# Moving the streamed operand of TensorE against its next weights in SBUF: many distances in place of two

## The chip, the cores and the metric

The kernel runs on one core of one Trainium2 chip. The metric is the device time of one execution in microseconds (us). TensorE multiplies: it loads a block of 128x128 weights (`lhsT`, the trace's LDWEIGHTS, engine PEld) and streams columns of a second operand (`rhs`, the trace's MATMUL, engine PE) past it into PSUM. VectorE (DVE) and ScalarE (ACT) do the elementwise work, SyncE (SP) issues the transfers between HBM and SBUF.

## The reference

```python
def sm_attn(qq, kk, vv):
    s = scale * np.matmul(qq, kk.transpose(0, 1, 3, 2))
    a = np.exp(s - np.max(s, axis=-1, keepdims=True))
    return np.matmul(a / (np.sum(a, axis=-1, keepdims=True) + 1e-09), vv)
...
x = sm_attn(q, sm_attn(p, k, v), same)        # 8 batches, 8 heads, 576 tokens, 32 packs, head 64
x = x.reshape(4608, 512)
h = x @ w_in1                                 # 512 -> 2048
x = np.where(h > 0, h, np.exp(np.minimum(h, 0)) - 1) @ w_out1
h = x @ w_in2                                 # second MLP, 512 -> 2048 -> 512
P = a[0] + a[1]*h + a[2]*h**2 + a[3]*h**3
Q = 1 + abs(b[0])*abs(h) + abs(b[1])*h**2
out = (P / (Q + 1e-6)) @ w_out2
```

## The kernel before

Every large product is kept to float32 accuracy by splitting each operand into a high and a low part (float32r, four bytes each) and adding three matmuls: high x high, high x low, low x high. All those matmuls have a full 128x128 weight block of their own, so there is one weight load for each matmul.

**First MLP** (the first half of the time). Eight batches of 576 tokens, each in two halves of 288 (`TA`). A half's attention result lies in `A_flat` as a high and a low part (`s2_hi`, `s2_lo`); three such slots follow each other, one for each half in turn. For each of 16 blocks of 128 hidden units, `a_h` streams 288 columns of `A_flat` past blocks of the tile `m` (6 matmuls, line 395), the activation makes the two parts of `g` in one of two slots of `gl_all` (`a_hi`, `a_lo`), and `a_o` streams those past blocks of the tile `wo` (12 matmuls, line 430). A step of 18 matmuls repeats 256 times, 32 steps a batch. Between them stand the attention matmuls of the next batch.

**Second MLP** (the second half). The tokens are taken as 6 groups of 384 columns (`TU`), and for each group 8 pairs of hidden blocks: 48 pairs in all. A pair needs seven products of a two-by-two scheme with seven multiplications (`prod`, line 698, 6 matmuls each): it streams 384 columns of an operand in one of eleven x slots (`xslot`; 0 to 4 are parts of one tile, `xs_wi`; 5 to 10 are tiles of their own) past blocks of the tile `sw`. The rational function makes four `g` tiles for a pair (`g_tile`, in `A_flat` for even pairs, in `A_flat`, `g1`, `g2` and `g3` for odd ones). In `out_mm` (line 774, 36 matmuls a pair) these `g` tiles are the weights, and 512 columns of `wo2` are streamed. One window of the plan holds the products of one pair and the output matmuls of the one before.

The order on each engine is written out by hand (`PLAN`, `LAST` and the tables of steps), so it does not depend on the numbers below.

**Distances.** SBUF addresses here are counted in four-byte words within a partition. In the built program the weight tiles `m`, `wo`, `sw` and the streamed `wo2` start 48 words past a multiple of 64; `A_flat` and `gl_all` start 16 words past one. All strides inside (320 in `A_flat` and `gl_all`, 384 in x, 128 and 512 in the weights) are multiples of 64 words. So the distance from a streamed operand's start to the start of the next weights, counted modulo 64, is the same for all matmuls of a kind. The constants that set it before are

```python
TP, OFA, OFG = 320, 4, 4
OFX, OFM = 4, 28
```

`OFA` and `OFG` shift the operands in `A_flat` and `gl_all`: 16 + 4 - 48 = -28, which is 36 modulo 64. `OFX` shifts x: 48 + 4 - 48 = 4. `OFM` shifts the `g` tiles, which are weights: 48 - (16 + 28) = 4. Where the kind changes, the distance differs once: from a product to an output matmul it is 52 - 44 = 8, from an output matmul to a product 48 - 48 = 0.

Of the kernel before, what the change touches and what calls it, by code (L numbers as in the profile page):

```python
# [11 lines left out]
F32R = mybir.dt.float32r  # L12
# [10 lines left out]
def packed_attention_moe_moe2_kernel(  # L23
# [23 lines left out]
    TA = S // 2  # L47
    NBLK = TA // 32
    NU = NT // 2
    TU = 384  # L50
# [24 lines left out]
    NWS = NF - 1  # L75


    TP, OFA, OFG = 320, 4, 4
    OFX, OFM = 4, 28

    P = ctx.enter_context(tc.tile_pool(name="P", bufs=1))
    dram = ctx.enter_context(tc.tile_pool(name="dram", bufs=1, space=bass.MemoryType.DRAM))
# [4 lines left out]
    T2 = actx.enter_context(tc.tile_pool(name="T2", bufs=1))  # L87
# [9 lines left out]

    T2.tile([128, 32], F32, tag="pad", name="pad")
    A_flat = T2.tile([128, 12 * TP + 64], F32R, tag="A", name="A_flat")
    A_all = A_flat[:, :12 * TP].rearrange("p (a b c x) -> p a b c x", a=3, b=2, c=2)  # L100
    gl_all = T2.tile([128, 4, TP], F32R, tag="gl", name="gl_all")
    n_A = [0]

    ident = P.tile([128, 128], F32, tag="ident", name="ident")
# [227 lines left out]

    def s2_hi(b, hf):
        d = st[b]
        A = d["A", hf] = A_all[:, n_A[0] % 3, :, :, OFA:OFA + TA]
        n_A[0] += 1
        nc.scalar.copy(A[:, 0], d["s2y", hf])

    def s2_lo(b, hf, eng=None):
        d = st[b]  # L340
        A, y = d["A", hf], d.pop(("s2y", hf))
        (eng or nc.vector).tensor_tensor(A[:, 1], y, A[:, 0].bitcast(F32), ALU.subtract)

# [26 lines left out]
    wi = [wi_all[:, c] for c in range(NC)]  # L370
# [15 lines left out]
    def a_h(s):  # L386
        b, n, f, _ = a_step(s)
        m = m_t[b, f // 4]
        A = st[b]["A", n]
        ps = ps_w.tile([128, 512], F32, tag="h", name=f"h_{s}", bufs=2)  # L390
        c0 = (f % 4) * 128
        i = 0
        for r in range(2):
            for wx, ax in ((0, 0), (0, 1), (1, 0)):
                nc.tensor.matmul(  # L395
                    ps[:, :TA], lhsT=m[:, wx, r, c0:c0 + 128], rhs=A[:, ax, r, :],
                    start=(i == 0), stop=(i == 5))
# [13 lines left out]

    def a_hi(s):
        d = mlp[s]
        d["ghi"] = gl_all[:, s % 2, OFG:OFG + TA]
        nc.scalar.copy(d["ghi"], d["g"])  # L415

    def a_lo(s):
        d = mlp[s]
        d["glo"] = gl_all[:, 2 + s % 2, OFG:OFG + TA]
        nc.vector.tensor_tensor(d["glo"], d["g"], d["ghi"].bitcast(F32), ALU.subtract)  # L420

    acc = None
# [231 lines left out]
    swt, wo2, xs, bst = {}, {}, {}, {}  # L654
# [15 lines left out]
    def xview(t):  # L670
        return t[:, :4 * TU].rearrange("p (h k t) -> p h k t", h=2, k=2)

    def xslot(n, j):
        i = (7 * n + j) % 11
        if i not in xs:
            if i < 5:
                t = P.tile([128, 20 * TU + OFX], F32R, tag="wi", name="xs_wi")
                xs.update((k, xview(t[:, OFX + 4 * TU * k:])) for k in range(5))
            else:
                tag = "q" if i == 10 else f"m{i - 5}"  # L680
                xs[i] = xview(P.tile([128, 4 * TU + OFX], F32R, tag=tag, name=f"xs_{i}")[:, OFX:])
        return xs[i]

    def x_load(n, j):
        if n >= NB2:
            return
        nc.sync.dma_start(out=xslot(n, j).bitcast(F32), in_=x2d[:, j, :, :, n * TU:(n + 1) * TU].bitcast(F32))

    m2 = {}

    def prod(p, j, bank, start):
        if p >= NPAIR:
            return
        w, x = swt[p, j // 2], xslot(p // NPR, j)
        i = 0
        for k in range(2):
            for wx, xx in ((0, 0), (0, 1), (1, 0)):
                nc.tensor.matmul(  # L698
                    m2["ab"][bank][:, :TU], lhsT=w[:, j % 2, wx, k, :], rhs=x[:, xx, k, :],
                    start=(start and i == 0), stop=(i == 5), skip_group_check=True)  # L700
                i += 1
# [53 lines left out]

    def g_tile(p, f, i):
        k = 2 * (1 - f) + i
        a = A_flat[:, OFM:OFM + 12 * TP].rearrange("p (a x) -> p a x", x=2 * TU)
        if p % 2 == 0:
            return a[:, (2, 3, 4, 1)[k]]  # L760
        return (a[:, 0], m2["g1"], m2["g2"], m2["g3"])[k] if k else a[:, 0]

    def r_hi(p, f):
        nc.scalar.copy(g_tile(p, f, 0), m2["t", f])  # L764

    def r_lo(p, f):
        nc.vector.tensor_tensor(g_tile(p, f, 1), m2["t", f], g_tile(p, f, 0).bitcast(F32), ALU.subtract)

    def out_mm(p, i, fs=(1, 0), ks=(0, 1, 2)):
        for f in fs:  # L770
            w = wo2[p, f]
            for k in ks:
                g, wx = ((0, 0), (0, 1), (1, 0))[k]
                nc.tensor.matmul(  # L774
                    acc[i], lhsT=g_tile(p, f, g)[:, i * 128:(i + 1) * 128], rhs=w[:, wx, :],
                    start=(p % NPR == 0 and f == 1 and k == 0),
                    stop=(p % NPR == NPR - 1 and f == 0 and k == 2))
# [86 lines left out]
    with tc.manual_schedule():  # L864
# [51 lines left out]
        V, A = nc.vector, nc.scalar  # L916
# [20 lines left out]
        for f in range(NWS, NF):  # L937
            t = P.tile([128, 2, 512], F32, tag=f"wo{f}", name=f"scr_wo{f}")
# [43 lines left out]
        s2_pe(0, 1, extra("s2x"))  # L982
        s2_tr(0, 0)
        s2_hi(0, 0)
        m_lo(0, 0, half(0)[0])
        s2_lo(0, 0, V)
# [21 lines left out]
        def s2_at(s, *a):  # L1008
            seq_at(s, a, (s2_pe, s2_max), s2_sub, s2_exp, s2_sum, s2_mul, s2_tr, s2_hi, s2_lo)
# [15 lines left out]
        NS = 2 * NF  # L1025
# [9 lines left out]
        for t, fn, *a in ((-2, m_hi, 0, 0, h1), (-2, m_lo, 0, 0, h1), (-2, c3, oo[0]), (-2, c4, oo[0], nc.gpsimd),  # L1035
                          (-2, s2_max, 0, 1), (-2, s2_sub, 0, 1, V),
                          (-1, s2_exp, 0, 1), (-1, c3, oo[1]), (-1, s2_sum, 0, 1), (-1, s2_mul, 0, 1, V),
                          (-1, c4, oo[1], V),
                          (0, c3, oo[2]), (0, c4, oo[2], nc.gpsimd), (0, s2_tr, 0, 1), (0, s2_hi, 0, 1),
                          (0, s2_lo, 0, 1, V)):  # L1040
            at(ewq, t, fn, *a)
        for p in seq[NKD + 1:]:
            t = when[p]
# [14 lines left out]
        for b in range(B - 1):  # L1058
            o, n = b * NS, b + 1
# [33 lines left out]
        for i in range(4):  # L1093
            c, kt = divmod(i, 2)
            s = NS * (1 + i)
            a21, a22, a11, a12 = ("i", c + 2, kt), ("i", c + 2, kt + 2), ("i", c, kt), ("i", c, kt + 2)
            s1, s2, s3, s4 = (("s", i, j) for j in range(1, 5))
            ta, tb = ("cc", "cb") if i % 2 else ("cb", "cc")
# [21 lines left out]
        for i, (b, s, u, t) in enumerate(slots):  # L1120
            f = i // 2 + NPR * (i % 2)
# [3 lines left out]
        def b_open():  # L1125
            t1x.close()
            tb = t2x.enter_context(tc.tile_pool(name="TB", bufs=1, reuse_waits="tile"))
            for f in (1, 0):
                for t in ("w", "sq", "t"):
                    m2[t, f] = tb.tile([128, 2 * TU], F32, tag=f"{t}{f}", name=f"{t}_{f}")  # L1130
            for t in ("s1", "u2"):
                m2[t] = tb.tile([128, TU], F32, tag=t, name=t)
            m2["h1"] = tb.tile([128, 2, TU], F32, tag="h1", name="h1")
            m2["g3"] = tb.tile([128, 2 * TU + 32], F32R, tag="g3", name="g3")[:, OFM:OFM + 2 * TU]
            psm[0].close()
            ps_ab = psm[0].enter_context(
                tc.tile_pool(name="ps_ab", bufs=1, space=bass.MemoryType.PSUM, reuse_waits="tile"))
            m2["ab"] = [ps_ab.tile([128, 512], F32, tag=f"bank{i}", name=f"bank{i}") for i in range(2)]
            k = P.tile([128, 2 * TU + 3 * DM], F32, tag="k", name="h0_o")
            m2["h0", 0] = k[:, :2 * TU].rearrange("p (a t) -> p a t", a=2)  # L1140
            m2["o"] = [k[:, 2 * TU + DM * i:2 * TU + DM * i + DM] for i in range(3)]

        def b_rest():
            v = P.tile([128, 6 * TU + 32 + OFM], F32R, tag="v", name="xg_v")
            xs[9] = xview(v[:, OFX:])
            m2["g2"] = v[:, 4 * TU + 32 + OFM:]
            m2["g1"] = P.tile([128, 2 * TU + 32 + OFM], F32R, tag="wo15", name="g1")[:, 32 + OFM:]
            m2["h0", 1] = T2.tile([128, 2, TU], F32, tag="gl", name="h0")
            t = P.tile([128, 2, DM], F32, tag="wo14", name="o34")
            m2["o"] += [t[:, i] for i in range(2)]  # L1150
            acc[:0] = [ps_w.tile([128, 512], F32, tag="h", name=f"acc_h{i}", bufs=2) for i in range(2)]

        t2x = ExitStack()
        o = NA - NS
# [4 lines left out]
        for t in range(4):  # L1159
            at(ldq, o + 20 + t, s_load, 0, t)  # L1160
            at(ldq, o + 24 + t, s_load, 1, t)
        at(ldq, o + 24, b_open)
        for i in range(2):
            at(ldq, o + 26 + 2 * i, wo2_load, i)
# [3 lines left out]
        for s in range(-2, NA):  # L1168
# [13 lines left out]
            if 0 <= s + 1 < NA:  # L1182
                a_hi(s + 1)
                lo = functools.partial(a_lo, s + 1)
# [13 lines left out]
            if s >= 0 and a_step(s)[3][1] and a_evac(s):  # L1198
                prep, n = x_prep(s), a_step(s)[1] if s < NA - 1 else 2
                for i, ops in zip(XSTEPS[n][::2], XSTEPS[n][1::2]):  # L1200
                    for op in ops.split():
                        t = s + 1 + i
# [4 lines left out]
        for _ in mix:  # L1207
            pass
        run(ewq, NA)
        b_rest()  # L1210
        for s in range(NPAIR):
            for _ in window(s):
# [58 lines left out]
```

## Time and profile before

| what | value |
|---|---|
| median of 2 runs | 1491.83 us (1491.42 to 1492.24) |
| the profiled execution: its time / its span | 1491.81 us / 1490.0 us |
| mean granted TensorE clock | 0.998 of full speed (2.4 GHz) |
| matmuls with float32r operands: lines 430, 395, 698, 774 | 3072, 1536, 2016, 1728 |

The span runs from the first to the last instruction; the 1.8 us outside it are not in the trace. A matmul's busy time in the trace includes the time its columns need to pass through the array, and neighbours overlap; what a matmul costs is therefore read as the time from its start to the start of the next, from the start times of the timeline.

### The profile page before, as it was taken

The page shows a single profiled execution, that of the slowest core. Times are in us where ns is not written, and L with a number is a line of the kernel's source. Part 1 is how long each engine was busy: PE and PEld are TensorE (multiplying, and loading weights), DVE is VectorE, ACT ScalarE, POOL GpSimd, SP SyncE. Part 2 cuts the span into 40 slices and gives each one's busy share as a digit, 9 for nine tenths or more (in the row PEclk, how much of TensorE's full clock was granted, in tenths as well). Part 3 has the DMA queues.
Part 4 walks back from the last instruction along what each step waited for, and adds up shares of the span by engine and source line. Part 5 has one row for each costly group of instructions (what it writes and reads, how often), then busy time and mean ns, then how long its engine had stood idle before and what let it go on. Part 6 is the DMA issues. An engine that isn't in the chain of part 4 may idle for free.

```text
span 1490.0 us, 26768 instructions
## 1 busy us (share of the span) xinstructions
PE 1458.7 (98%) x10188; PEld 1325.0 (89%) x10188; DVE 1246.5 (84%) x2078; ACT 1087.1 (73%) x1992; POOL 3.3 (0%) x8
## 2 busy tenths in 40 slices
PE   7899999999999999999999999999999999999997
PEld 5778989999898999999989999999999999999996
DVE  6888687777877687776699999999999999999997
ACT  4876667676777667677778787787777778778775
POOL 0000000000000000000000000000000000000000
PEclk9999999999999999999999999999999999999999
DMA  9542555465555445467967877777677777777641
GB/s 355 177 150 62 172 149 169 127 184 154 154 164 157 149 146 162 137 204 236 326 193 258 296 226 254 259 233 236 223 257 237 249 262 223 257 257 226 203 143 56
DMA packets 191264, 301.14 MB, mean 202 GB/s; under 512 B 13472, under 2 KB 131488, under 8 KB 190240
## 3 DMA queue, kind: packets, MB, share of 16 engines
q1 hardware_dynamic: 190528, 298.51, 62.1%
q8 instruction: 81, 1.33, 0.4%
q10 hardware_dynamic: 608, 0.92, 0.2%
q14 instruction: 47, 0.39, 0.1%
HBM read 233.84 MB, written 65.54 MB: 201 GB/s over the span
## 4 chain that ended last, share of the span: by engine, by line
PE 85%; DMA 5%; DVE 5%; ACT 4%; issue 1%; SPq 0%; ACTq 0%; DVEq 0%
PE bank L698 23%; PE acc L430 22%; PE acc L774 17%; PE h L395 11%; PE acc_h L774 8%; PE m L351 2%; DMA x2d<-x 1%; DMA x2d<-xpart 1%; DMA raw0('o', 6)_134<-in_w_out_dram 1%; PE pp L252 1%; DVE g L410 1%; DMA raw0('o', 2)_118<-in_w_out_dram 1%; DMA s2d<-w2('i', 2, 2)_cb 1%; DMA v<-in_v_dram 1%; ACT g L405 0%
## 5 line engine op out<-in xcount | busy, mean ns | idle before, releaser
L430 PE MATMUL acc<-gl_all,wo 128*128 128x288 f32 x3072 | 454.1, 296 | 10.0 <-DVE gl_all L420 3.9
L430 PEld LDWEIGHTS acc<-gl_all,wo 128*128 128x128 f32 x3072 | 413.5, 188 | 54.0 <-ACT g L405 17.6
L395 PE MATMUL h<-A_flat,m 128*128 128x288 f32 x1536 | 242.9, 293 | 2.0 <-DVE m L365 0.9
L395 PEld LDWEIGHTS h<-A_flat,m 128*128 128x128 f32 x1536 | 214.9, 188 | 3.9 <-DVE m L365 1.6
L774 PE MATMUL acc<-wo,A_flat 128*128 128x512 f32 x768 | 200.8, 389 | 0.0
L698 PE MATMUL bank<-xs_wi,sw 128*128 128x384 f32 x960 | 191.3, 337 | 0.2 <-DVE h L716 0.2
L698 PE MATMUL bank<-xs,sw 128*128 128x384 f32 x912 | 180.9, 338 | 2.7 <-DVE h L716 2.6
L698 PEld LDWEIGHTS bank<-xs_wi,sw 128*128 128x128 f32 x960 | 171.2, 188 | 8.9 <-DVE h L716 0.7
L750 DVE SCALAR_TENSOR_TENSOR w<-w,sq 128x768 f32<-128x768 f32 x192 | 178.7, 950 | 0.1
L410 DVE SCALAR_TENSOR_TENSOR g<-g,h 128x288 f32<-128x288 f32 x256 | 115.7, 452 | 75.4 <-ACT g L405 73.3
L415 ACT CAST gl_all<-g 128x288 fp32r<-128x288 f32 x256 | 110.6, 432 | 90.2 <-PE acc L430 61.6
L698 PEld LDWEIGHTS bank<-xs,sw 128*128 128x128 f32 x912 | 162.6, 188 | 11.4 <-DVE h L716 3.7
L420 DVE TENSOR_TENSOR gl_all<-g,gl_all 128x288 fp32r<-128x288 f32 x256 | 115.6, 452 | 61.3 <-ACT gl_all L415 60.6
L774 PEld LDWEIGHTS acc<-wo,A_flat 128*128 128x128 f32 x768 | 142.5, 188 | 19.3
L404 ACT ACTIVATE g<-h 128x288 f32<-128x288 f32 x256 | 105.1, 411 | 48.4 <-PE h L395 47.9
L405 ACT ACTIVATE g<-g 128x288 f32<-128x288 f32 x256 | 113.9, 445 | 8.1
L774 PE MATMUL acc_h<-wo,A_flat 128*128 128x512 f32 x384 | 102.6, 390 | 0.0
L754 DVE SCALAR_TENSOR_TENSOR t<-t,cf,w 128x768 f32<-128x768 f32 x96 | 97.4, 1015 | 1.7
L732 DVE SCALAR_TENSOR_TENSOR w<-sq,cf,w 128x768 f32<-128x768 f32 x96 | 97.5, 1015 | 1.7
L743 ACT ACTIVATE sq<-w,cf 128x768 f32<-128x768 f32 x96 | 89.7, 934 | 1.6 <-DVE w L732 1.6
L746 ACT ACTIVATE sq<-sq,cf 128x768 f32<-128x768 f32 x96 | 89.7, 934 | 1.6
L764 ACT CAST A_flat<-t 128x768 fp32r<-128x768 f32 x72 | 60.4, 838 | 37.1 <-DVE t L754 37.0
(419 smaller groups left out, 1950.9 us busy)
## 6 DMA issues: line engine op xcount, KB each, us to landing
sw<-s2d SPq DMA_DIRECT2D x144, 512.0 KB, 4.2
wo<-wo2d SPq DMA_DIRECT2D x96, 512.0 KB, 5.1
x2d<-x SPq DMA_DIRECT2D x210, 144.0 KB, 2.4
xs_wi<-x2d SPq DMA_DIRECT2D x20, 768.0 KB, 7.5
xs<-x2d SPq DMA_DIRECT2D x19, 768.0 KB, 7.5
sw<-s2d SPq DMA_DIRECT2D x48, 256.0 KB, 2.8
q<-in_qT_dram SPq DMA_DIRECT2D x16, 576.0 KB, 5.5
v<-in_v_dram SPq DMA_DIRECT2D x8, 1024.0 KB, 6.7
```

What stands on the lines that cost most here:

```text
L395: nc.tensor.matmul(ps[:, :TA], lhsT=m[:, wx, r, c0:c0 + 128], rhs=A[:, ax, r, :], start=(i == 0), stop=(i == 5))
L404: nc.scalar.activation(d["e"], d["h"][:, :TA], AF.Exp)
L405: nc.scalar.activation(d["e"], d["e"], AF.Relu, scale=-1.0, bias=1.0)
L410: nc.vector.scalar_tensor_tensor(d["g"], d["e"], -1.0, d["h"][:, :TA], ALU.mult, ALU.max)
L415: nc.scalar.copy(d["ghi"], d["g"])
L420: nc.vector.tensor_tensor(d["glo"], d["g"], d["ghi"].bitcast(F32), ALU.subtract)
L430: nc.tensor.matmul(acc[m][:, :TA], lhsT=w[:, wx, m * 128:(m + 1) * 128], rhs=d[g], start=(first and i == 0), stop=(last and i == 2))
L698: nc.tensor.matmul(m2["ab"][bank][:, :TU], lhsT=w[:, j % 2, wx, k, :], rhs=x[:, xx, k, :], start=(start and i == 0), stop=(i == 5), skip_g ...
L732: nc.vector.scalar_tensor_tensor(w, m2["sq", f], cf[:, 5:6], w, ALU.mult, ALU.add)
L750: nc.vector.scalar_tensor_tensor(w, w, c, m2["sq", f], ALU.add, ALU.mult)
L754: nc.vector.scalar_tensor_tensor(t, t, cf[:, 0:1], m2["w", f], ALU.add, ALU.mult)
L774: nc.tensor.matmul(acc[i], lhsT=g_tile(p, f, g)[:, i * 128:(i + 1) * 128], rhs=w[:, wx, :], start=(p % NPR == 0 and f == 1 and k == 0), st ...
```

## The change

The four constants become tables. Nothing else changes: the built program has the same instructions in the same order on every engine, with the same waits, and all tiles start where they did; only the places of operands inside `A_flat`, `gl_all`, the x slots and the `g` tiles move, each by a multiple of 4 words.

```diff
-    TP, OFA, OFG = 320, 4, 4
-    OFX, OFM = 4, 28
+    TP = 320
+    OFA = (4, 12, 20, 32, 40, 44, 52, 60)
+    OFG = (4, 12, 20, 32, 24, 28, 16, 8)
+    OFX = (8, 12, 16, 20, 24, 28, 32, 36, 44, 52, 60)
+
+    def ofm(p):
+        return 4 * (p // 2 % 8) + (0 if p % 2 else 32)
...
-    gl_all = T2.tile([128, 4, TP], F32R, tag="gl", name="gl_all")
+    gl_all = T2.tile([128, 4 * TP], F32R, tag="gl", name="gl_all")
+
+    def A_part(b, i):
+        t = A_flat[:, OFA[b]:OFA[b] + 12 * TP].rearrange("p (a b c x) -> p a b c x", a=3, b=2, c=2)
+        return t[:, i, :, :, :TA]
+
+    def gl_part(s, i):
+        o = OFG[s // NS] + TP * i
+        return gl_all[:, o:o + TA]
...
-        A = d["A", hf] = A_all[:, n_A[0] % 3, :, :, OFA:OFA + TA]
+        A = d["A", hf] = A_part(b, n_A[0] % 3)
...
-        d["ghi"] = gl_all[:, s % 2, OFG:OFG + TA]
+        d["ghi"] = gl_part(s, s % 2)
...
-                t = P.tile([128, 20 * TU + OFX], F32R, tag="wi", name="xs_wi")
-                xs.update((k, xview(t[:, OFX + 4 * TU * k:])) for k in range(5))
+                t = P.tile([128, 20 * TU + OFX[4]], F32R, tag="wi", name="xs_wi")
+                xs.update((k, xview(t[:, OFX[k] + 4 * TU * k:])) for k in range(5))
...
     def g_tile(p, f, i):
         k = 2 * (1 - f) + i
-        a = A_flat[:, OFM:OFM + 12 * TP].rearrange("p (a x) -> p a x", x=2 * TU)
-        if p % 2 == 0:
-            return a[:, (2, 3, 4, 1)[k]]
-        return (a[:, 0], m2["g1"], m2["g2"], m2["g3"])[k] if k else a[:, 0]
+        o = ofm(p)
+        if p % 2 == 0 or k == 0:
+            o += 2 * TU * (0 if p % 2 else (2, 3, 4, 1)[k])
+            return A_flat[:, o:o + 2 * TU]
+        return m2[f"g{k}"][:, o:o + 2 * TU]
```

The distances modulo 64, in words:

| streamed, next weights | before | after |
|---|---|---|
| `A_flat`, `m` (line 395), batches 0 to 7 | 36 | 36, 44, 52, 0, 8, 12, 20, 28 |
| `gl_all`, `wo` (line 430), batches 0 to 7 | 36 | 36, 44, 52, 0, 56, 60, 48, 40 |
| x slots 0 to 10, `sw` (line 698) | 4 | 8, 12, 16, 20, 24, 28, 32, 36, 44, 52, 60 |
| `wo2`, `g` of even pairs 0, 2, 4, ... (line 774) | 4 | 0, 60, 56, 52, 48, 44, 40, 36, and again |
| `wo2`, `g` of odd pairs 1, 3, 5, ... | 4 | 32, 28, 24, 20, 16, 12, 8, 4, and again |

Together the rows of after hold all sixteen multiples of 4.

## Rows read from the trace of the kernel before

**Rows 1.** The page: busy time, share of the span and instructions of each engine.

```profile
PE 1458.7 (98%) x10188; PEld 1325.0 (89%) x10188; DVE 1246.5 (84%) x2078; ACT 1087.1 (73%) x1992; POOL 3.3 (0%) x8
```

**Rows 2.** Windows, all engines: busy us and instructions, then clock, DMA share, GB/s.

```profile
core 0: us, PE busy (x) PEld busy (x) DVE busy (x) ACT busy (x) POOL busy (x), PEclk, DMA share, GB/s
...
306.00:392.00 86.00, 86.00 (x793) 78.78 (x793) 66.08 (x149) 60.23 (x144) 0.00 (x0) 1.00 0.53 155
392.00:478.00 86.00, 86.00 (x796) 78.99 (x795) 66.19 (x149) 60.36 (x145) 0.00 (x0) 1.00 0.54 160
```

**Rows 3.** Windows of the second MLP, the same columns.

```profile
830.00:930.00 100.00, 100.00 (x504) 90.83 (x503) 92.72 (x111) 80.22 (x112) 0.00 (x0) 1.00 0.76 253
930.00:1030.00 100.00, 100.00 (x503) 90.85 (x503) 92.37 (x111) 76.71 (x108) 0.00 (x0) 1.00 0.72 238
...
1330.00:1430.00 100.00, 100.00 (x503) 90.92 (x503) 92.98 (x111) 78.35 (x110) 0.00 (x0) 1.00 0.69 227
```

**Rows 4.** Timeline of PE, first MLP: start us, us, engine, line, operation.

```profile
701.27 1.72 PE L430 MATMUL acc<-gl_all,wo 128*128 128x288 f32 x12
702.83 0.94 PE L395 MATMUL h<-A_flat,m 128*128 128x288 f32 x6
703.61 1.72 PE L430 MATMUL acc<-gl_all,wo 128*128 128x288 f32 x12
```

**Rows 5.** Timeline of PE, one window of the second MLP.

```profile
999.71 1.22 PE L698 MATMUL bank<-xs_wi,sw 128*128 128x384 f32 x6
1000.76 1.52 PE L774 MATMUL acc_h<-wo,A_flat 128*128 128x512 f32 x6
1002.13 1.22 PE L698 MATMUL bank<-xs_wi,sw 128*128 128x384 f32 x6
...
1006.95 2.27 PE L698 MATMUL bank<-xs,sw 128*128 128x384 f32 x12
1009.06 2.88 PE L774 MATMUL acc<-wo,A_flat 128*128 128x512 f32 x12
1011.78 1.22 PE L698 MATMUL bank<-xs,sw 128*128 128x384 f32 x6
...
1014.19 1.21 PE L698 MATMUL bank<-xg_v,sw 128*128 128x384 f32 x6
1015.25 1.04 PE L698 MATMUL bank<-xs_wi,sw 128*128 128x384 f32 x5
```

**Rows 6.** Timeline of PEld (weight loads), the same stretch.

```profile
1000.59 1.27 PEld L774 LDWEIGHTS acc_h<-wo,A_flat 128*128 128x128 f32 x6
```

**Rows 7.** Lines by form, PE: busy us, mean ns, idle us before.

```profile
L430 PE MATMUL acc<-gl_all,wo 128*128 128x288 f32 x3072 | 454.1, 296 | 10.0 <-DVE gl_all L420 3.9 <-ACT gl_all L415 2.7 <-ACT xpart L454 1.2
L395 PE MATMUL h<-A_flat,m 128*128 128x288 f32 x1536 | 242.9, 293 | 2.0 <-DVE m L365 0.9 <-ACT A_flat L337 0.7 <-DVE A_flat L342 0.5
L698 PE MATMUL bank<-xs,sw 128*128 128x384 f32 x912 | 180.9, 338 | 2.7 <-DVE h L716 2.6
```

**Rows 8.** Timeline of PE at a transpose of the attention (line 229).

```profile
153.33 0.60 PE L229 MATMUL t<-ident,E 128*128 128x128 f32 x4
153.76 0.27 PE L230 MATMUL t<-ident,E 128*64 128x128 f32 x1
```

More of the change, by code (lines that the diff above doesn't have):

```diff
@@ L99, in packed_attention_moe_moe2_kernel @@
     A_flat = T2.tile([128, 12 * TP + 64], F32R, tag="A", name="A_flat")
-    A_all = A_flat[:, :12 * TP].rearrange("p (a b c x) -> p a b c x", a=3, b=2, c=2)
-    gl_all = T2.tile([128, 4, TP], F32R, tag="gl", name="gl_all")
+    gl_all = T2.tile([128, 4 * TP], F32R, tag="gl", name="gl_all")
[5 more added lines that the diff above has]
+        return gl_all[:, o:o + TA]
     n_A = [0]
@@ L418, in a_lo @@
         d = mlp[s]
-        d["glo"] = gl_all[:, 2 + s % 2, OFG:OFG + TA]
+        d["glo"] = gl_part(s, 2 + s % 2)
         nc.vector.tensor_tensor(d["glo"], d["g"], d["ghi"].bitcast(F32), ALU.subtract)
@@ L676, in xslot @@
             if i < 5:
-                t = P.tile([128, 20 * TU + OFX], F32R, tag="wi", name="xs_wi")
-                xs.update((k, xview(t[:, OFX + 4 * TU * k:])) for k in range(5))
+                t = P.tile([128, 20 * TU + OFX[4]], F32R, tag="wi", name="xs_wi")
+                xs.update((k, xview(t[:, OFX[k] + 4 * TU * k:])) for k in range(5))
             else:
                 tag = "q" if i == 10 else f"m{i - 5}"
-                xs[i] = xview(P.tile([128, 4 * TU + OFX], F32R, tag=tag, name=f"xs_{i}")[:, OFX:])
+                xs[i] = xview(P.tile([128, 4 * TU + OFX[i]], F32R, tag=tag, name=f"xs_{i}")[:, OFX[i]:])
         return xs[i]
@@ L1133, in b_open @@
             m2["h1"] = tb.tile([128, 2, TU], F32, tag="h1", name="h1")
-            m2["g3"] = tb.tile([128, 2 * TU + 32], F32R, tag="g3", name="g3")[:, OFM:OFM + 2 * TU]
+            m2["g3"] = tb.tile([128, 2 * TU + 32], F32R, tag="g3", name="g3")
             psm[0].close()
@@ L1143, in b_rest @@
         def b_rest():
[L1144 to L1147, printed above, removed]
+            v = P.tile([128, 6 * TU + 128], F32R, tag="v", name="xg_v")
+            xs[9] = xview(v[:, OFX[9]:])
+            m2["g2"] = v[:, 4 * TU + 96:]
+            m2["g1"] = P.tile([128, 2 * TU + 64], F32R, tag="wo15", name="g1")[:, 32:]
             m2["h0", 1] = T2.tile([128, 2, TU], F32, tag="gl", name="h0")
```

## Prediction

> **What bounds the kernel now.** I read the shares of the engines first. TensorE is busy 98% of the span, its weight loads 89% [rows 1]. Since a busy TensorE can still hide waits, the windows come next: in two neighbouring stretches of the first MLP, and in every window of the second, PE is busy the whole time at granted clock 1.00, the 2.4 GHz level, while DVE has 66 of 86 us and 92 to 93 of 100 us [rows 2, 3]. The second MLP issues 503 or 504 matmuls in each 100 us whatever DVE and ACT do in them [rows 3]; the idle time before the two kinds of the first MLP is 12 us in all and before the products 2.7 us [rows 7]. So the time is a sum of matmul spacings, and what the change does to a spacing goes into the time one to one, with 12 to 15 us at most in which a slower matmul could fill a wait.
>
> The spacings come from the start times. First MLP: 18 matmuls from 701.27 to 703.61 are 2.34 us, 130.0 ns each [rows 4]. Products: 12 in 2.11 us and 6 in 1.05 or 1.06, 175 to 176.5 ns. Outputs: 12 in 2.72 us, 226.7 ns [rows 5]. From 288 to 512 columns the spacing grows by 96.7 ns, 0.43 ns a column; one column per cycle at 2.4 GHz is 0.417. So the columns take 120, 160 and 213 ns, and the rest, 10, 15.5 and 13.5 ns a matmul, is there beside each load. The load of the next weights does run beside the stream: the first load for the outputs starts at 1000.59, 0.17 us before the matmul that uses it at 1000.76, which is where the product before it starts [rows 5, 6]. This remainder is the only thing the change can act on through the distance.
>
> **The change part by part.** No instruction is added, removed or moved and no wait is new, so no transfer and no elementwise operation is later than before except by TensorE's own pace. The elementwise writes and the x transfers land at other places; 93 of 100 us of DVE are beside PE [rows 3], so a few per cent there would stay covered, and beyond 7% DVE would take over the second MLP. I cost them at nothing. What changes is the distance at 2,688 + 1,344 = 4,032 matmuls of the first MLP (seven of eight batches), at 2,016 products and at nearly all 1,728 outputs: 7,776 in all.
>
> What the trace says of other distances is little, but it is not nothing. The last product of a group that is followed by outputs has distance 8 where the others have 4: such a group of 6 takes 1.05 us, and the group of 6 followed by another product 1.06 [rows 5]. The last output before a product has distance 0 instead of 4: six take 1.37 us, twelve 2.72 us, 228 and 227 ns each [rows 5]. With one matmul in six different, a difference of more than some 10 ns in that one would show. So distances 0 and 8 cost what 4 costs, within 10 ns. Distance 36 is only seen at 288 columns, where the remainder is 10 ns, against 13.5 and 15.5 at 4. The other twelve distances are in no row.
>
> The bounds for these come from the two remainders. Above: the first MLP's matmuls take the product's 15.5 ns in place of 10, 5.5 ns x 4,032 = +22 us, and the second MLP, which is there already, stays. Below: the second MLP takes 10 ns, -5.5 ns x 2,016 - 3.5 ns x 1,728 = -17 us, and the first stays. That is 1514 and 1475 against the profiled execution's 1491.8, which is also the median of the runs to 0.02 us. I take half of each, since the new distances spread over all sixteen places and no row is nearer to one end: +11 - 8.5 = +2.5, **1494 us**.
>
> The Trainium skill's page "SBUF — State Buffer", section "Who interferes with whom", gives TensorE two independent read ports, one for the moving operand and one for weight loads, and says that TensorE never waits on anyone. By that rule the distance would be worth nothing and the sum would be 1491.8. The remainders above do not decide it: they show a cost beside the load, and not that it depends on the place.
>
> **The rivals.**
>
> *The place is worth nothing.* The remainder belongs to loading weights under a stream as such. For it: distances 0, 4 and 8 alike [rows 5], and spacings that repeat to 0.01 us through the half of the kernel in which three other engines write to SBUF. Against it: 10 ns at one distance and 13.5 to 15.5 ns at another, with nothing in the number of columns that would order them (288, 512, 384). Time: 1491.8, within 3. This is what the page's rule amounts to.
>
> *Sustained collisions.* Load and stream both walk through their words in order. If both take a word per cycle, a distance that puts them in the same part of the memory puts them there for the whole load, and they would take turns. The price: 128 words at 0.417 ns, 53 ns for each such matmul. For it: only four distances are seen, so twelve places could be bad. Against it: 0, where the two start at the same place modulo 64, shows nothing of the kind. If two of the sixteen distances are bad, 7,776 / 8 x 53 ns = +52 us, **1544**; if four, 1596. It decides from a mean of 3.8 ns over the 7,776, that is, from a little over one bad distance in sixteen. TensorE would be the place, and in the second MLP the bad ones would show as single x slots or single pairs.
>
> *Two distances that happen to be poor.* The remainder could be a collision already, absent elsewhere. For it: the transposes of the attention, whose distance is 48, take 0.43 us for 4, 108 ns each, where two cycles for each of their 128 columns are 106.7 [rows 8]. Against it: their loads are of another kind, and 0, 4, 8 and 36 all have the remainder. Going from 10, 15.5 and 13.5 to 2 ns would be worth 8 x 4,032 + 13.5 x 2,016 + 11.5 x 1,728 = 79 us at all distances, 40 at half of them: **1452**. DVE at 93% of the second MLP would still leave room for that [rows 3].
>
> The Trainium skill's page "TensorE: Matmul & The Clock Gate", section "Wait — 56ns, not 53.3ns?", puts the gap between streamed matmuls at the columns over 2.4 GHz plus about 2.5 ns. Its gaps here would be 122.5, 162.5 and 215.8 ns, all under the spacings of the trace; an estimate with that page's remainder at every changed matmul gives some 75 us less than now, 1417.
>
> *The change does not act as written*, for instance by a wait between operands that now overlap in `A_flat`. The built programs have the same waits, so this has next to no weight: 0.02.
>
> **How the numbers follow.** Mixed small effects, 1475 to 1514, 0.40: the forecast, 1494. The place is worth nothing, 1492: 0.25. Sustained collisions, 1515 to 1600 with most of it under 1550: 0.25. Poor places now, 1413 to 1475: 0.08. The last: 0.02. Two per cent of 1492 are 30 us, which is about what a measurement of this kernel can tell from no change. Faster by more than that (below 1462) needs most of the poor-place case: 0.07. Slower (above 1522) has nearly all of the collisions and some of the odd case: 0.26. Within: 0.67. The range for 8 in 10 runs from 1475, where the lower bound ends, to 1545, the collisions at two places: it leaves out the poor-place case and about half of the collisions.
>
> **What the profile of the changed kernel would show.** Batch 0 of the first MLP keeps its distances, so its step must stay at 2.34 us; if it does not, the cause is not the distance. With the forecast, the steps of the batches lie between 2.32 and 2.44 us (129 to 135.5 ns), groups of six products between 1.02 and 1.06 us, of six outputs between 1.34 and 1.37, and each x slot keeps its own value in all 48 windows. If the place is worth nothing, all of these are as before and windows take 15.53 us. With collisions, a few batches, slots or pairs stand out by tens of ns a matmul (a step of up to 3.3 us, a group of six products of up to 1.37) and the others stay. With poor places now, some fall to about 2.20 us a step. The forecast is wrong if the mean over the sixteen places is far from the places in use, in either direction: four distances seen of sixteen are a thin base, and that is its weakest step.

## The result: 1% slower

The changed kernel takes 1506.66 us (median of 2 runs, 1506.05 to 1507.27) against 1491.83 us: a ratio of 1.0102, 95% interval 1.0085 to 1.0118. That is inside the range of the prediction and within 2%; the forecast of 1494 had the sign and too small a size. The profiled execution took 1507.27 us with a span of 1505.5 us, 15.5 us more than the one of before.

The page's line of the engines, after the change, has the same instruction counts as [rows 1], with 17 us more in PE, 0.1 us in DVE and 1 us in ACT:

```profile
PE 1475.5 (98%) x10188; PEld 1334.1 (89%) x10188; DVE 1246.6 (83%) x2078; ACT 1088.2 (72%) x1992; POOL 3.3 (0%) x8
```

Windows of the second MLP after the change (busy us and instructions of PE, PEld, DVE, ACT, POOL, then the clock):

```profile
842.00:942.00 100.00, 100.00 (x499) 90.05 (x498) 91.96 (x110) 77.44 (x108) 0.00 (x0) 1.00 0.73 246
942.00:1042.00 100.00, 100.00 (x498) 89.97 (x497) 90.90 (x109) 77.25 (x108) 0.00 (x0) 1.00 0.70 237
```

PE is as full as in [rows 3], at the same granted clock, but issues 498 or 499 matmuls in 100 us in place of 503 or 504. The timeline of PE after the change: first a step's end in batch 0, whose distances are as before, then a whole step of batch 2 (distance 52), the first products of the second MLP, and a part of one window of the second MLP:

```profile
118.13 1.72 PE L444 MATMUL acc<-gl_all,wo 128*128 128x288 f32 x12
119.69 0.94 PE L409 MATMUL h<-A_flat,m 128*128 128x288 f32 x6
...
253.29 0.96 PE L409 MATMUL h<-A_flat,m 128*128 128x288 f32 x6
254.09 1.76 PE L444 MATMUL acc<-gl_all,wo 128*128 128x288 f32 x12
255.69 0.96 PE L409 MATMUL h<-A_flat,m 128*128 128x288 f32 x6
...
725.06 1.37 PE L712 MATMUL bank<-xs_wi,sw 128*128 128x384 f32 x7
...
1015.88 1.56 PE L789 MATMUL acc<-wo,A_flat 128*128 128x512 f32 x6
1017.27 2.28 PE L712 MATMUL bank<-xs,sw 128*128 128x384 f32 x12
1019.39 2.93 PE L789 MATMUL acc<-wo,A_flat 128*128 128x512 f32 x12
1022.15 1.22 PE L712 MATMUL bank<-xs,sw 128*128 128x384 f32 x6
```

The first product before the change; then groups of matmuls of one form (count, busy us, mean ns, idle us before), one of the outputs before, and both kinds of the first MLP, the same outputs and one group of products after:

```profile
717.46 1.22 PE L698 MATMUL bank<-xs_wi,sw 128*128 128x384 f32 x6
```

```profile
L774 PE MATMUL acc<-wo,A_flat 128*128 128x512 f32 x768 | 200.8, 389 | 0.0
```

```profile
L444 PE MATMUL acc<-gl_all,wo 128*128 128x288 f32 x3072 | 461.5, 299 | 8.1 <-ACT gl_all L429 2.8 <-DVE gl_all L434 2.3 <-ACT xpart L468 1.2
L409 PE MATMUL h<-A_flat,m 128*128 128x288 f32 x1536 | 245.9, 295 | 2.0 <-DVE m L379 0.9 <-ACT A_flat L351 0.7 <-DVE A_flat L356 0.5
L789 PE MATMUL acc<-wo,A_flat 128*128 128x512 f32 x768 | 204.6, 394 | 0.0
L712 PE MATMUL bank<-xs,sw 128*128 128x384 f32 x912 | 181.1, 338 | 2.5 <-DVE h L730 2.5
```

In batch 0 twelve matmuls take 1.56 us, 130.0 ns each, as in [rows 4]. In batch 2 a step is 2.40 us, 133.3 ns each. In the second MLP twelve products take 2.12 us, 176.7 ns, against 175.8 [rows 5]; twelve outputs 2.76 us, 230.0 ns, and six 1.39 us, 231.7 ns, against 226.7 [rows 5]. So the time came in two nearly equal parts: the first product starts 7.6 us later (725.06 against 717.46 us), and the rest, 8 us, is 0.16 us more for each of the 48 windows of the second MLP. The first of the two numbers is uncertain by some 2 to 3 us: in the seven profiled executions of this document that leave the first MLP as it was, the first product starts between 715.2 and 720.2 us. By the groups, the two kinds of the first MLP take 7.4 and 3.0 us more busy time than in [rows 7] and this group of outputs 3.8 us more, while the products take 0.2 us more. Products cost nothing; it is the steps of the first MLP and the outputs.

### The profile page after: what moved, and what is told of

Same layout as the page of the kernel before. It is cut to its first block, busy times and chain, and to the rows that moved or that the text cites. A ratio compares the mean times of both kernels' runs of the same rounds, so it can differ in the third digit from the quotient of the medians.

```text
span 1505.5 us, 26768 instructions
## 1 busy us (share of the span) xinstructions
PE 1475.5 (98%) x10188; PEld 1334.1 (89%) x10188; DVE 1246.6 (83%) x2078; ACT 1088.2 (72%) x1992; POOL 3.3 (0%) x8
## 4 chain that ended last, share of the span: by engine, by line
PE 87%; DVE 5%; ACT 4%; DMA 3%; issue 1%; SPq 0%; ACTq 0%; DVEq 0%
PE acc L444 23%; PE bank L712 22%; PE acc L789 17%; PE h L409 11%; PE acc_h L789 9%; PE m L365 2%; DMA x2d<-x 1%; PE pp L266 1%; DMA q<-in_qT_dram 1%; PE s1h L200 1%; DVE g L424 0%; DMA raw0('i', 0, 1)_99<-in_w_in_dram 0%; DMA wo2d<-whi('o', 10)_7848 0%; PE s L300 0%; DVE w L764 0%
## 5 line engine op out<-in xcount | busy, mean ns | idle before, releaser
L444 PE MATMUL acc<-gl_all,wo 128*128 128x288 f32 x3072 | 461.5, 299 | 8.1 <-ACT gl_all L429 2.8
L444 PEld LDWEIGHTS acc<-gl_all,wo 128*128 128x128 f32 x3072 | 419.8, 189 | 52.3 <-ACT g L419 18.4
L789 PE MATMUL acc<-wo,A_flat 128*128 128x512 f32 x768 | 204.6, 394 | 0.0
L768 DVE SCALAR_TENSOR_TENSOR t<-t,cf,w 128x768 f32<-128x768 f32 x96 | 97.4, 1015 | 1.7
L746 DVE SCALAR_TENSOR_TENSOR w<-sq,cf,w 128x768 f32<-128x768 f32 x96 | 97.4, 1014 | 1.6
```

Source lines behind the costliest of these rows:

```text
L444: nc.tensor.matmul(acc[m][:, :TA], lhsT=w[:, wx, m * 128:(m + 1) * 128], rhs=d[g], start=(first and i == 0), stop=(last and i == 2))
L746: nc.vector.scalar_tensor_tensor(w, m2["sq", f], cf[:, 5:6], w, ALU.mult, ALU.add)
L768: nc.vector.scalar_tensor_tensor(t, t, cf[:, 0:1], m2["w", f], ALU.add, ALU.mult)
L789: nc.tensor.matmul(acc[i], lhsT=g_tile(p, f, g)[:, i * 128:(i + 1) * 128], rhs=w[:, wx, :], start=(p % NPR == 0 and f == 1 and k == 0), st ...
```

## The experiments

Three theories of a matmul's spacing were open. **Distance**: it depends on the distance of the matmul's own kind. **Place**: it depends on where an operand starts, whatever the other does. **Neighbours**, later called carry-over: it also depends on what ran before it. A spacing in what follows is the mean over the matmuls named, from start times; means over a whole kernel leave out the few spacings with a wait in them.

**Everything 8 words further, distances kept.**

```diff
+    P.tile([128, 8], F32, tag="pad0", name="pad0")
     ident = P.tile([128, 128], F32, tag="ident", name="ident")
```

> The kernel before with one pad of 8 words ahead of all tiles: every operand lies 8 words further, all distances stay (36 and 4). Distance theory: the time of before, ratio within 0.2% of 1, steps of 130.0 ns and outputs of 226.7 ns. Place theory (what counts is where each operand starts, not how they stand to each other): a changed kernel's cost, a ratio of 1.005 to 1.015, outputs at 230 ns or more.

1491.36 us against 1491.89, ratio 0.9996 (0.9986 to 1.0005). Its timeline of PE:

```profile
701.83 1.72 PE L431 MATMUL acc<-gl_all,wo 128*128 128x288 f32 x12
703.39 0.94 PE L396 MATMUL h<-A_flat,m 128*128 128x288 f32 x6
704.17 1.72 PE L431 MATMUL acc<-gl_all,wo 128*128 128x288 f32 x12
...
1040.82 2.88 PE L775 MATMUL acc<-wo,A_flat 128*128 128x512 f32 x12
1043.54 0.69 PE L699 MATMUL bank<-xs,sw 128*128 128x384 f32 x3
```

A step is 2.34 us and twelve outputs are 2.72 us, the numbers of [rows 4, 5]. Where the operands lie is worth nothing as long as all move together by 8 words; the place theory falls for such a shift.

**A map of distances**, a kernel of nothing but matmuls with their loads, twelve in a group; DVE and ACT are idle beside them.

```diff
+    for n, d in ((288, 320), (512, 512)):
+        for iw in range(16):
+            for ix in range(16):
...
+                for m in range(4):
+                    for wx, g in ((0, 0), (0, 1), (1, 0)):
+                        w0, x0 = 4 * iw + 512 * wx + 128 * m, 4 * ix + d * g
+                        nc.tensor.matmul(t[:, :n], lhsT=W[:, w0:w0 + 128], rhs=X[:, x0:x0 + n], ...
```

> Leaves out the whole computation: only groups of 12 matmuls with their weight loads, streamed start and weights start each at all sixteen multiples of 4 words, once with 288 and once with 512 columns. Distance theory: all groups with the same difference cost the same, some 130 to 134 ns (288) and 227 to 234 ns (512), and the lowest of 288 is at difference 36, of 512 at 4. Place theory: rows or columns of the map agree and diagonals do not. Neighbour theory (the added cost comes from changing between distances): with one distance through a group, all groups alike within 1 ns.

Timeline of PE in the map; in a name like `s_n_e`, `s` is 288 columns (`l` 512), the next letter the streamed start in steps of 4 words (a = 0, n = 52), the last the weights' start (e = 16, f = 20, j = 36). The last group, `l_h_j`, is shown in its two halves, and then the start of the one after it:

```profile
136.08 1.77 PE L67 MATMUL s_l_e<-X,W 128*128 128x288 f32 x12
137.69 1.76 PE L67 MATMUL s_m_e<-X,W 128*128 128x288 f32 x12
139.29 1.73 PE L67 MATMUL s_n_e<-X,W 128*128 128x288 f32 x12
140.85 1.76 PE L67 MATMUL s_o_e<-X,W 128*128 128x288 f32 x12
...
163.02 1.72 PE L67 MATMUL s_m_f<-X,W 128*128 128x288 f32 x12
164.58 1.76 PE L67 MATMUL s_n_f<-X,W 128*128 128x288 f32 x12
...
836.94 2.91 PE L67 MATMUL l_f_j<-X,W 128*128 128x512 f32 x12
839.69 2.96 PE L67 MATMUL l_g_j<-X,W 128*128 128x512 f32 x12
842.49 1.56 PE L67 MATMUL l_h_j<-X,W 128*128 128x512 f32 x6
843.89 1.52 PE L67 MATMUL l_h_j<-X,W 128*128 128x512 f32 x6
845.25 2.88 PE L67 MATMUL l_i_j<-X,W 128*128 128x512 f32 x12
```

Twelve matmuls at distance 28 (`s_l_e`) take 1.61 us, 134 ns each; at 36 (`s_n_e`) 1.56 us, 130. With the weights 4 words further, the same distance (`s_m_f`, 48 - 20 = 28) takes 1.56 us, 130 ns. So distance 28 costs 134 ns with weights at a multiple of 8 words and 130 ns with weights 4 words past one. With 512 columns and weights at 36, a streamed start at 24 (`l_g_j`, distance 52) takes 2.80 us, 233 ns, and one at 20 (`l_f_j`, distance 48) 2.75, 229. This holds over the whole map: groups with the same distance and the same remainder of the weights' start by 8 words mostly agree to half a ns once the first two rows of weights are over, and the two remainders give two different lists. The place theory falls, as it wanted rows or columns of the map to agree, and so does a cost of changing distances alone, as groups that hold one distance each still differ by up to 8 ns. By medians of these, 288 columns take 130.2 (distance 36) to 134.1 ns (28) with weights at multiples of 8, and 130.1 (28) to 133.3 (36) with the others; 512 columns 227.2 (60) to 234.9 (52), and 226.7 (28 and 60) to 233.3 (52), with 228.1 at 4, where the lowest was expected. The lists are not those of the distance alone, though. In the map a group follows one whose distance is 4 less, always the same one but for the first of each row of weights, and the group `l_h_j` (distance 56) takes 1.40 us for its first six, 233.3 ns each, and 1.36 us for its last six, 226.7 each. The same fall stands in every group of 512 columns at distances 40 and 56 with weights 4 words past a multiple of 8, so the 230 ns that the lists have at these two is in part what ran before. Neither list goes below 130 and 226.7 ns. So the remainder over the columns, 10 and 13.5 ns, is not removed at any of them; the distances of before sit on the floor of the list in the first MLP and near it for the outputs.

**The table of the g tiles alone**, and **the tables of the first MLP alone** (the other tables set back to the constants of before).

```diff
-    OFA = (4, 12, 20, 32, 40, 44, 52, 60)
-    OFG = (4, 12, 20, 32, 24, 28, 16, 8)
-    OFX = (8, 12, 16, 20, 24, 28, 32, 36, 44, 52, 60)
+    OFA = (4,) * 8
+    OFG = (4,) * 8
+    OFX = (4,) * 11
```

> Only the table of the g tiles is changed, all else as before. Distance theory: outputs at some 232 ns as in the changed kernel, +8 us, ratio 1.0055; products and first MLP as before. Neighbour theory, with the x slots as the neighbours that count: outputs stay under 229 ns, ratio under 1.002.

1500.86 us, ratio 1.0064 (1.0049 to 1.0079): +9 us; outputs at 232.0 ns in the mean of their starts (227.0 before), products at 175.4, the first MLP at 130.0. Outputs under 229 ns, which the neighbour theory wanted, did not come.

```diff
-    OFX = (8, 12, 16, 20, 24, 28, 32, 36, 44, 52, 60)
+    OFX = (4,) * 11
...
-        return 4 * (p // 2 % 8) + (0 if p % 2 else 32)
+        return 28
```

> Only the two tables of the first MLP are changed. Distance theory: the steps of batches 1 to 7 as in the changed kernel, 131 to 134 ns a matmul, +8 us, ratio 1.0055, the second MLP as before. Neighbour theory: batches 1 to 3, in which both operands of a step have the same distance, fall back to 130 ns, and only batches 4 to 7 stay above; +4 us.

1499.21 us, ratio 1.005 (1.0035 to 1.0065): +7.3 us. Batch 2, where both operands have distance 52, is at 133 ns here too, and batches 1 and 3 at 131.4 to 131.8; so different neighbours are not needed for a cost.

**The x slots' table alone**, the part for which the changed kernel's products showed no cost.

```diff
-    OFA = (4, 12, 20, 32, 40, 44, 52, 60)
-    OFG = (4, 12, 20, 32, 24, 28, 16, 8)
+    OFA = (4,) * 8
+    OFG = (4,) * 8
...
-        return 4 * (p // 2 % 8) + (0 if p % 2 else 32)
+        return 28
```

> Only the table of the x slots is changed. Distance theory: products as in the changed kernel, 173 to 177 ns by slot and 175 in the mean, outputs at 227 ns, so no change: ratio 0.999 to 1.001. Neighbour theory: outputs above 229 ns because the products beside them have other distances, +4 us or more, ratio over 1.002.

1496.25 us, ratio 1.0032 (1.0022 to 1.0041), +5 us, which the distance theory excluded. Products stay at 175.5 ns; the outputs, whose own distance is 4 as before, rise to 229.3. Its timeline of PE from 1228.0 to 1232.6 us:

```profile
1228.55 2.91 PE L789 MATMUL acc<-wo,A_flat 128*128 128x512 f32 x12
1231.30 1.22 PE L712 MATMUL bank<-xs_wi,sw 128*128 128x384 f32 x6
```

and the same stretch of the same kernel from 1229.7 us on, which keeps the last eight of the twelve:

```profile
1229.48 1.98 PE L789 MATMUL acc<-wo,A_flat 128*128 128x512 f32 x8
```

The first four outputs after the products take 0.93 us, 232.5 ns each; the last eight 1.82 us, 227.5 each. This group is a marked one: over all 45 groups of twelve outputs in this run the first four take 230.2 ns and the last eight 228.0. The run `x16_g0` further on, with one place for all products and one for all outputs, shows it with nothing mixed; here is one of its groups of twelve, as three and nine:

```profile
1225.93 0.85 PE L789 MATMUL acc<-wo,A_flat 128*128 128x512 f32 x3
1226.62 2.20 PE L789 MATMUL acc<-wo,A_flat 128*128 128x512 f32 x9
1228.66 1.20 PE L712 MATMUL bank<-xs_wi,sw 128*128 128x384 f32 x6
```

The first three take 0.69 us, 230 ns each, and the other nine 2.04 us, 226.7 each; over its 45 such groups the first four spacings are 229.2, 232.5, 230.8 and 226.7 ns, and all later ones 226.6 or 226.7. So a group of outputs starts slow after products at another distance and comes to its own value after three or four matmuls; in the map it took six. A matmul's spacing carries over.

**Whose weights?** The second part of another map alternates the weights between two places 8e words apart and keeps the distance 36 either to a matmul's own weights (`o`) or to the next (`n`); its first part maps the products.

```diff
+                for k in range(24):
+                    w0 = (8 * e) * (k % 2)
+                    x0 = (w0 if own else 8 * e - w0) + 36
```

> Leaves out the whole computation. First part: the products' order of six matmuls with 384 columns, streamed start and weights start each at all sixteen multiples of 4 words, 12 matmuls a group. Distance theory: spacing set by the difference and by whether the weights start at a multiple of 8 words, between some 172 and 178 ns, with the difference 4 near 175.5 and at least one under 174. Second part: 24 matmuls with 288 columns, weights alternating between two places 8e words apart (e = 0 to 7). In groups o the streamed start keeps 36 words to its own weights, in groups n to the next weights. If the next weights count: n groups all at 130 to 130.5 ns, o groups at 132 to 133 for e of 1 to 3. If a matmul's own weights count: the other way round. If neither, both alike.

Timeline of PE (the letter after `o` or `n` is e, a = 0; the last one counts the two rounds):

```profile
583.58 3.39 PE L79 MATMUL n_b_a<-X,W 128*128 128x288 f32 x24
586.81 3.36 PE L79 MATMUL n_c_a<-X,W 128*128 128x288 f32 x24
590.00 3.29 PE L79 MATMUL n_d_a<-X,W 128*128 128x288 f32 x24
593.13 3.36 PE L79 MATMUL n_e_a<-X,W 128*128 128x288 f32 x24
...
609.08 3.29 PE L79 MATMUL o_b_b<-X,W 128*128 128x288 f32 x24
612.20 3.37 PE L79 MATMUL o_c_b<-X,W 128*128 128x288 f32 x24
615.41 3.35 PE L79 MATMUL o_d_b<-X,W 128*128 128x288 f32 x24
...
634.44 3.39 PE L79 MATMUL n_b_b<-X,W 128*128 128x288 f32 x24
637.67 2.56 PE L79 MATMUL n_c_b<-X,W 128*128 128x288 f32 x18
```

`n_b` takes 3.23 us (134.6 ns) in both rounds and `n_d` 3.13 (130.4), though the distance to the next weights is 36 in both; `o_b` takes 3.12 (130.0) and `o_c` 3.21 (133.8), though the distance to their own weights is 36. Neither distance alone sets the spacing; the two rounds agree to 0.2 ns, so it is not chance. In the first part the products lie between 173.2 (distance 28) and 179.0 ns (60) with weights at multiples of 8, and 4 costs 175.0.

**A map of combinations.** Products and outputs in the kernel's order, 48 matmuls for each pair of an x place and a g place, counted from the start of the weights and of `wo2`; the kernel before has x at 4 and g at 60.

```diff
+    for ig in range(16):
+        for ix in range(16):
...
+            for np_, no in ((2, 2), (1, 1), (1, 1)):
+                for j in range(np_):
+                    six(t, 4 * ix, j)
+                for j in range(no):
+                    outs(u, 4 * ig, j + np_)
```

> Leaves out the whole computation. Products and outputs of the second MLP in groups of 12, 12, 6, 6, 6, 6, in the kernel's order of operands, one x place and one g place for a group of 48, all 256 combinations. If spacing belongs to each kind's own distance: the products' mean depends on the x place alone and the outputs' on the g place alone, each by one column of numbers, within 0.5 ns. If a matmul's delay carries over into the next ones: outputs of the same g place differ by 2 ns and more with the x place, as they did in the run with the x table alone, and the place of before (x at 4, g at 60) gives 175.4 and 227.0 ns. A combination under 174 and at most 227 ns would beat the places of before by some 3 us in the kernel.

Timeline of PE: the first row of a group of 48 and the first of the group after it, for x at 56 and g at 0, for x at 60 and g at 32, and for the places of before:

```profile
152.11 2.25 PE L70 MATMUL p_o_a<-X,W 128*128 128x384 f32 x12
...
161.73 1.06 PE L70 MATMUL p_p_a<-X,W 128*128 128x384 f32 x5
...
1414.79 2.31 PE L70 MATMUL p_p_i<-X,W 128*128 128x384 f32 x12
...
1424.64 0.69 PE L70 MATMUL p_a_j<-X,W 128*128 128x384 f32 x3
...
2371.93 2.27 PE L70 MATMUL p_b_p<-X,W 128*128 128x384 f32 x12
...
2381.60 0.69 PE L70 MATMUL p_c_p<-X,W 128*128 128x384 f32 x3
```

The groups take 9.62, 9.85 and 9.67 us. Without the first six products of each group, whose neighbours belong to the group before, and scaled to 42 products and 36 outputs in 48 windows, the places of before give 747.1 us, the mean of all 256 combinations 754.0, the best (x at 56, g at 0: 173.9 and 226.9 ns) 742.6, the worst 766.6. With g at 0 the outputs lie between 226.5 and 231.3 ns by the x place alone: carry-over again. For the places of before the map has 175.3 and 227.9 ns, where 175.4 and 227.0 were expected from the kernel: its outputs are 0.9 ns too slow there.

**Three combinations put into the kernel**, all with the first MLP of before.

```diff
-    OFX = (4,) * 11
+    OFX = (56,) * 11
...
-        return 28
+        return 32
```

The second has 16 in place of 56; the third has 60, and returns 0.

> Distances of before in the first MLP; products all at 56, outputs all at 0. Carry-over theory with the map of combinations: products 173.9 ns, outputs 226.9 ns, 4.5 us less, ratio 0.997. If a kind's own distance alone counts, by the means over the other place: products 174.8 ns, outputs 229.3 ns, +3 us, ratio 1.002.

> Products all at 16, outputs all at 0. Carry-over theory with the map of combinations: products 173.3, outputs 228.6 ns, 2.8 us less, ratio 0.998. Own distance alone: products 173.8, outputs 229.3 ns, no change.

> One distance for each kind again, but a poor pair: products at 60, outputs at 32. Both theories with the map: products 177 to 179 ns, outputs 232.5 ns, +13 us, ratio 1.0085. Mixing alone as the cause (any single distance is as good as the one before): 1.000.

| x distance, g distance | ratio to before, 95% interval | products, outputs in the trace | combinations' map said |
|---|---|---|---|
| 56, 0 | 0.9978 (0.9969 to 0.9987) | 174.0, 226.9 ns | 173.9, 226.9 |
| 16, 0 | 0.999 (0.9981 to 0.9999) | 173.3, 228.8 | 173.3, 228.6 |
| 60, 32 | 1.0084 (1.007 to 1.0098) | 177.7, 231.9 | 177.3, 232.7 |

One window of the second MLP, of the first of these and then of the last:

```profile
842.00:942.00 100.00, 100.00 (x506) 90.83 (x505) 93.08 (x111) 80.60 (x113) 0.00 (x0) 1.00 0.72 237
```

```profile
842.00:942.00 100.00, 100.00 (x495) 89.98 (x494) 90.02 (x107) 78.48 (x110) 0.00 (x0) 1.00 0.70 227
```

506 matmuls in 100 us against 503 or 504 [rows 3] and 495. The first beats both kernels, 1488.38 us in the median against 1491.69 before, and it does so with the outputs at a place that costs 229.3 ns in the mean over the x places of the map of combinations. Its 3.3 us are less than the 4.5 expected, and the second takes 1.3 us less where 2.8 were expected: the map had the outputs of before too slow. In the kernel the first's outputs are at 226.9 ns against 227.0 before, so its gain is in the products, 174.0 against 175.4. The third takes 12.4 us more, where 13 were expected; that a single distance is always as good as the one before falls with it.

## Why the prediction was right, and where it was off

**What bounds the kernel.** Right: it is a sum of spacings on TensorE. The slower spacings come to 17 us by the terms below and the span is 15.5 us longer; part of the rest filled waits, as the prediction allowed (the idle time before the matmuls with `wo` fell from 10.0 [rows 7] to 8.1 us). DVE and ACT have the same busy time to 1 us. Two readings were a little off without bearing on the sum: one window of the second MLP (1030 to 1130 us) issues 505 matmuls, and in its first 100 us PE is busy 97.4 us, not the whole time.

**Mixed small effects.** Right as the likeliest case: 1506.66 us lies in its 1475 to 1514. The sixteen places differ by some 4 ns of 130, 6 ns of 175 and 8 ns of 227 in the maps, not by tens. "Sustained collisions" at 53 ns a matmul falls: no group shows one. "The place is worth nothing" falls too, with an interval well away from 1, and poor places now falls with lists that end at 130 and 226.7 ns. The prediction took 30 us as about what a measurement can tell from no change; the interval here is 2.5 us to either side.

**The first MLP's term.** +11 us was taken; the trace has +1.9 ns at 1,536 and +2.0 ns at 3,072 matmuls, 9 us, of which 7.6 us show at the end of the stage. Right in sign and size; the map's 130.1 to 134.1 ns is what its bound of 15.5 ns remainder allowed. That bound was the remainder of matmuls with 384 columns, and half of it was taken for want of a nearer row, so that the size came out is in part luck.

**The second MLP's term.** This is the step that was mis-sized, with the wrong sign: -8.5 us was taken, half of a gain of 17, and +8 us came. It rested on the sentence that the second MLP "is there already" as an upper bound. It was not: the outputs' 226.7 ns is at the floor of the map (226.7), not at its top (234.9), so most other places cost more; they rose by 4.7 ns x 1,728 = 8.1 us. The products, at 175.0 inside the map's 173.2 to 179.0, moved by -0.15 ns where half of 5.5 was taken. Two remainders of matmuls with different column counts don't bound each other. The forecast of +2.5 us was thus the sum of a term about right and one with the wrong sign; about half of the measured +15 us is a loss in the second MLP that the upper bound of 1514 held to be impossible, so that the time lies under that bound is in part luck too.

**"Distances 0 and 8 cost what 4 costs, within 10 ns."** True within its 10 ns, and too coarse to carry the middle of the range: everything that came is 2 to 8 ns a matmul. It was also read from one matmul at another distance among neighbours at the old one. The last output before a product has distance 0 in both kernels; it cost 226.8 ns in the mean before and 230.4 after, with other neighbours. In groups of their own in the map, 512 columns take 228.1 ns at 4 with weights 4 words past a multiple of 8, as the `g` tiles of before are, and 229.9 at 0 with weights at a multiple of 8, as `sw` is.

**The two rules weighed.** The page "SBUF — State Buffer" of the Trainium skill ("Who interferes with whom") has two independent read ports for TensorE, which waits on nobody. By that rule the place would be worth nothing; here the distance between its two reads moves the kernel by -0.2% to +1.0% with nothing else changed, so the measurement differs from what the rule would give, and decides. Whether the ports are where the delay arises is not shown. The page "TensorE: Matmul & The Clock Gate" of the Trainium skill ("Wait — 56ns, not 53.3ns?") has the columns over 2.4 GHz plus about 2.5 ns for the gap of streamed matmuls, by estimate 122.5 ns for 288 columns and 215.8 for 512; the lists of the map end at 130 and 226.7 ns, so its 2.5 ns were not had at any of the places tried.

**Parts.** Alone, the three tables cost 7.3, 9 and 5 us, together 21 against 15. The x table's 5 us are slower outputs, and outputs that are at 232.0 ns by their own table don't get slower by it again: in the changed kernel, with both tables, they are at 231.7.

**What stays open.** Which part of the SBUF or of TensorE makes a load and a stream delay each other was not found. Shown is what it depends on, for starts at multiples of 4 words: the distance modulo 64 words, whether the weights start at a multiple of 8 words, and what ran a few matmuls before; and that neither the distance to the next weights nor that to a matmul's own is enough. A shift of all operands by 4 words was not tried in the kernel.

## What to carry to other kernels

When weights are loaded under a stream and TensorE is the bound, the places of the two operands in SBUF were worth from -0.2% to +1.0% here, at no instruction. Such a choice can't be made for one kind of matmul at a time or read from one odd matmul in a row; a small kernel that runs the real order of kinds at all combinations gave spacings that held to within 0.9 ns in the full kernel. That is enough to tell a poor pair from a good one and too coarse to size a gain of 3 us. A scan that gives each batch or slot its own value pays the mean of the scan and mixes neighbours, so it answers less than it seems to.

## What was not expected of the hardware

A matmul's spacing has a memory: after products at another distance, outputs at an unchanged one start at 229 to 233 ns and come to 226.7 after three (`x16_g0`); in the map it takes six (`l_h_j`). Moving the weights by 4 words exchanges good and bad distances (28 takes 134 or 130 ns for 288 columns), moving everything by 8 words does nothing (0.9996). And the spacings repeat to a few tenths of a nanosecond: the outputs' mean is 226.98 ns before, 226.96 with the shift and 226.94 with the tables of the first MLP alone, though DVE is busy 92 to 93 of 100 us beside them [rows 3].
